# Routing products in rounded halves, one key buffer, and later ranks in a fused attention, MLP and MoE kernel

## The chip, the cores and the metric

The kernel runs on one core of a Trainium2 chip. The metric is the device time of one execution in microseconds (us). Five engines matter: TensorE (PE, matrix products), VectorE (DVE), ScalarE (ACT), GpSimdE (POOL) and SyncE (SP), whose queue here issues most of the DMA transfers. A matrix product reads a stationary operand (loaded as weights, PEld in the rows) and a moving operand, and accumulates in PSUM.

## The reference

```python
# r, k, v: (4, 8, 768, 48) f32; w, u: (8, 48); attention with a decaying state
for t in range(S):
    cur = einsum('bhd,bhe->bhde', u[None] * kt, vt)
    y[:, :, t] = einsum('bhd,bhde->bhe', rt, state + cur)
    state = w[None, :, :, None] * state + einsum('bhd,bhe->bhde', kt, vt)
# x = y as (3072, 384): one row for each token
x = (relu(x @ w_in) ** 2) @ w_out                 # w_in (384, 2048), w_out (2048, 384)
noisy = x @ w_gate + log1p(exp(x @ w_noise)) * noise   # (3072, 8)
top2, weights = best_two_of(noisy), softmax_over_the_two
out[rows] += weight * (relu(x[rows] @ w1[e]) @ w2[e])  # 8 experts, (384, 1024), (1024, 384)
```

## The kernel before, in words

**Tiling.** The 3072 tokens are 24 chunks of 128 rows, or 6 blocks (j = 0 to 5) of 512 tokens. The 384 features are three pieces (d = 0, 1, 2) of 128. Most products run on pairs of rounded numbers: an operand is a rounded high part (type fp32r) plus a rounded low part, and a product is hi*hi + hi*lo + lo*hi. Attention and routing use plain fp32 operands, of which the profile records every product as two passes.

**Stages.** A written-out list of steps (HEAD) does the attention of chunks 0 to 3 and begins the conversion of the MLP's weights into such pairs. Then comes the loop over blocks j and, in it, over 16 pieces f of the MLP's width: `mm1(j, f)` (line 501, nine products of 512 columns into `ph`, two buffers), `gsplit(j, f)` (lines 507 to 513: ACT takes relu, its square `g` and the rounded square `gh`; DVE takes `gl` = g - gh), and `mm2(j, f-2)` (line 524, nine products into `xo`, a single buffer of three PSUM banks). Behind `mm2(j-1, 15)`, in f = 1 of block j, comes `finish(j-1)` (line 531): it copies `xo` from PSUM to `x2T`, d = 0 and 2 on ACT, d = 1 on DVE. After the blocks come the experts, in units of token columns, with products of 264 to 512 columns (lines 806, 857, 889).

**What sets the order.** Nothing is scheduled at run time: each engine runs its own list in the order in which the program was written and waits on semaphores. Between `mm1` and `mm2` of each f lie two slots (32 for a block), each some nine products long. Tables give the place of every other step as a slot number with a fraction: CHUNKS for the attention of the next block, CONV_AT for the weights, ROUTE for the routing of the block before. ROUTE has three rows, of which the third is for j = 5.

**Routing.** `load_routing` (line 153) fills `gates`, 128 x 3 x 144: an identity, the gate weights and the noise weights. `r_row(j, i)` (line 549) takes the 128 tokens of chunk i: three fp32 products (line 557), with the token columns of `x2T` as weights and `gates` moving, give in one PSUM bank the transposed rows (128 columns for each d) and three partial logits (16 columns for each d). DVE adds the partial logits (`lz`, line 559), ACT copies the rows (line 560). A block has four such steps. Then DVE finds the two best experts, `r_rank` (line 658) counts places with three small products on PE, which wait for DVE's selection, and eight `r_send` scatter the rows from POOL.

**Keys.** `load(q, "k")` (line 200) brings chunk q's keys into `lk`, two buffers, from SP's queue; `pre(q)` (line 348) uses them: `pre_k` (line 370, `kp` = k * tk, on DVE for most chunks, on POOL for 4 to 8), then POOL multiplies r, k and u (line 357) and issues the load of k for chunk q + 2.

Of the kernel before, what the change touches and what calls it, by code (L numbers as in the profile page):

```python
# [8 lines left out]
F32 = mybir.dt.float32  # L9
F32R = mybir.dt.float32r  # L10
# [64 lines left out]
CLEAR = {3: (8.7, 14.7, 26.7), 4: (8.7, 14.7)}  # L75
# [18 lines left out]
def body(ctx, tc, r, k, v, w, u, w_in, w_out, w_gate, w_noise, noise, w1, w2, out):  # L94
# [58 lines left out]
    def load_routing():  # L153

        g = C["gates"] = consts.tile([P, KD, P + 2 * E], F32, name="gates")
        nc.gpsimd.tensor_copy(g[:, :, :P], ident[:, None, :].to_broadcast([P, KD, P]))
        nc.scalar.dma_start(g[:, :, P:P + E], w_gate.rearrange("(c p) e -> p c e", p=P))
        nc.scalar.dma_start(g[:, :, P + E:], w_noise.rearrange("(c p) e -> p c e", p=P))

# [25 lines left out]
    def load(q, names="rkv"):  # L185
# [3 lines left out]
        for nm in names:  # L189
            if nm == "r" and q < QD:  # L190
                t = rp[q % 2][:, :, :D]
            elif nm == "r":
                t = at.tile([P, H, D], F32, name="lr", tag="s3", bufs=1)
            elif nm == "k" and q == 0:
                t = kp[0][:, :, :D]
            elif nm == "v":
                t = at.tile([P, H, D], F32, name="lv", bufs=2)
            else:
                t = at.tile([P, H, D], F32, name="l" + nm, bufs=2)
            nc.sync.dma_start(t, SRC[nm][b, :, c * P:(c + 1) * P, :].rearrange("h s d -> s h d"))  # L200
            L.setdefault(q, {})[nm] = t
# [146 lines left out]
    def pre(q):  # L348
        a = A.setdefault(q, {})
        l = L[q]  # L350
        if q:
            pre_k(q)
        if q < QD:
            t = at.tile([P, H, D], F32, name="ra", bufs=2)
        else:
            t = at.tile([P, H, D], F32, name="rk", bufs=1)
        nc.gpsimd.tensor_mul(t, l["r"], l["k"])
        nc.gpsimd.tensor_mul(t, t, ub)
        a["rk"] = t
        load(q + 2, "k")  # L360

# [142 lines left out]
    def gsplit(j, f):  # L504
        ph = PH.pop((j, f))
        rt = m1.tile([P, BLK], F32, name="rt", bufs=1)
        nc.scalar.activation(rt, ph, AF.Relu)  # L507
        g = m1.tile([P, BLK], F32, name="g", bufs=1)
        nc.scalar.activation(g, rt, AF.Square)
        gh = m1.tile([P, BLK], F32R, name="gh", bufs=3)  # L510
        nc.scalar.activation(gh, rt, AF.Square)  # L511
        gl = m1.tile([P, BLK], F32R, name="gl", bufs=3)
        nc.vector.tensor_tensor(gl, g, gh.bitcast(F32), op=OP.subtract)  # L513
        G[j, f] = gh, gl
# [12 lines left out]
    def finish(j):  # L527
        xo = XO.pop(j)
        X2[j] = eb.tile([P, KD, BLK], F32, name="x2T", tag="s6", bufs=2)
        for d in range(KD):  # L530
            (nc.vector.tensor_copy if d == 1 else nc.scalar.copy)(X2[j][:, d, :], xo[:, d, :])

# [16 lines left out]
    def r_row(j, i):  # L549
        s = RT[j]  # L550
        if i == 0:
            s["lz"] = small("lz", [TPB, 2 * E])
        n = P + 2 * E
        pb = bank()[:, :KD * n].rearrange("p (d x) -> p d x", x=n)
        x = X2[j][:, :, i * P:(i + 1) * P]
        for d in range(KD):
            nc.tensor.matmul(pb[:, d, :], x[:, d, :], C["gates"][:, d, :], start=(d == 0), stop=(d == KD - 1),  # L557
                             skip_group_check=True)
        nc.vector.tensor_reduce(s["lz"][:, i, :], pb[:, :, P:].rearrange("p d e -> p e d"), axis=AX.X, op=OP.add)
        nc.scalar.copy(r_part(s, i), pb[:, :, :P])  # L560
# [440 lines left out]
    for j in range(NB):  # L1001
# [14 lines left out]
        if j == 0:  # L1016
            put(0.6, conv_w3, 2)
            for n in range(AW, 2 * NP):
                for at_, fn in zip(CONV_AT[n - AW], (conv_w1, conv_w2, conv_w3)):
                    put(at_, fn, n)  # L1020
            put(30.6, load_routing)
        if j == 1:
# [176 lines left out]
```

## Time and profile before

| | |
|---|---|
| median of 3 runs | 972.31 us (972.05 to 973.21) |
| the profiled execution | 972.28 us |
| its span, first to last instruction | 970.6 us |
| mean granted clock of TensorE | 0.989 |
| TensorE busy | 941.2 us, 97% |
| VectorE, ScalarE, GpSimdE busy | 543.2, 437.3, 351.3 us |

The profiled execution spends 1.7 us around its span and stands at the median of the runs. Ends of TensorE's records are modelled and products overlap, so the pace of a stretch is read from the starts: the distance from one start to the next is what a product costs. A number in brackets at the end of a row of the timeline is the idle time of that engine before it, with the instruction that ended it.

### The profile page before, as it was taken

The numbers are of one execution on the slowest core, as the hardware profiler recorded it, in microseconds if no ns is written. First come the engines' busy times: TensorE is split into PE (matmuls) and PEld (weight loads), VectorE is DVE, ScalarE is ACT, GpSimd is POOL, SyncE is SP. The second block draws the span as 40 slices with busy tenths as digits, with TensorE's granted clock in tenths as the row PEclk, the third lists the DMA queues.
The fourth block names the chain that finished last, engine by engine and source line by source line (L and its number), as shares of the span: only waits on it lengthen the run. The fifth ranks groups of instructions, "written<-read, shape, count | busy, mean of one in ns | idle before, by whom it ended". The sixth has DMA issues, their size and how long they took to land.

```text
span 970.6 us, 17617 instructions
## 1 busy us (share of the span) xinstructions
PE 941.2 (97%) x6816; PEld 812.9 (84%) x6816; DVE 543.2 (56%) x986; ACT 437.3 (45%) x797; POOL 351.3 (36%) x407
## 2 busy tenths in 40 slices
PE   6898999999999999999999999999999999999995
PEld 5676787878878878877878899989999898989985
DVE  6899955545855673683344563554545454456320
ACT  4666754434344444353555542443434444444220
POOL 5555552464563354455030353132121212212112
PEclk7999999999999999999999999999999999999998
DMA  7645449943343364442025268376555555654112
GB/s 170 162 132 151 138 121 288 271 128 82 76 114 72 87 160 131 109 98 83 0 99 127 75 141 181 96 141 135 115 101 124 103 112 118 119 101 89 21 21 36
DMA packets 193365, 112.35 MB, mean 116 GB/s; under 512 B 131792, under 2 KB 185840, under 8 KB 193264
## 3 DMA queue, kind: packets, MB, share of 16 engines
q1 hardware_dynamic: 181840, 91.22, 37.2%
q0 software_dynamic: 10624, 19.74, 11.1%
q8 instruction: 65, 1.06, 0.5%
q14 instruction: 36, 0.29, 0.1%
q10 hardware_dynamic: 800, 0.02, 0.0%
HBM read 74.83 MB, written 36.12 MB: 114 GB/s over the span
## 4 chain that ended last, share of the span: by engine, by line
PE 84%; DVE 8%; DMA 2%; ACT 2%; issue 1%; SPq 1%; POOL 0%; POOLq 0%; ACTq 0%; DVEq 0%
PE ph L806 19%; PE xo L524 17%; PE ph L501 17%; PE y L857 13%; PE y L889 4%; PE att L439 4%; PE ph L889 2%; PE att L421 2%; PE att L557 2%; PE y L806 2%; DVE t L276 1%; DVE t L275 1%; DMA stg<-in_moe_w_in 1%; DVE t L274 1%; DVE gl L513 1%
## 5 line engine op out<-in xcount | busy, mean ns | idle before, releaser
L868 POOL DMA_INDIRECT out<-yt,id x56 | 87.1, 1556 | 309.1 <-ACT yt L866 271.3
L513 DVE TENSOR_TENSOR gl<-g,gh 128x512 fp32r<-128x512 f32 x96 | 80.7, 841 | 145.2 <-ACT gh L511 141.9
L843 DVE SCALAR_TENSOR_TENSOR hl<-ph,hh 128x512 fp32r<-128x512 f32 (+1 forms) x112 | 66.6, 598 | 117.9 <-ACT hh L842 117.7
L507 ACT ACTIVATE rt<-ph 128x512 f32<-128x512 f32 x96 | 57.2, 595 | 157.8 <-PE ph L501 157.8
L806 PE MATMUL ph<-xh,w0h 128*128 128x512 f32 (+1 forms) x336 | 119.3, 355 | 0.0
L501 PE MATMUL ph<-x1h,wih 128*128 128x512 f32 x288 | 117.7, 409 | 1.3 <-ACT rt L507 0.7
L806 PE MATMUL ph<-xh,w0l 128*128 128x512 f32 (+2 forms) x336 | 116.8, 348 | 0.0
L806 PE MATMUL ph<-xl,w0h 128*128 128x512 f32 (+2 forms) x336 | 116.5, 347 | 0.2 <-DVE xl L783 0.2
L524 PE MATMUL xo<-gh,woh 128*128 128x512 f32 x288 | 114.7, 398 | 0.0
L524 PE MATMUL xo<-gh,wol 128*128 128x512 f32 x288 | 112.4, 390 | 0.9 <-POOL wol L289 0.9
L501 PE MATMUL ph<-x1l,wih 128*128 128x512 f32 x288 | 112.7, 391 | 0.1
L501 PE MATMUL ph<-x1h,wil 128*128 128x512 f32 x288 | 112.3, 390 | 0.0
L524 PE MATMUL xo<-gl,woh 128*128 128x512 f32 x288 | 112.3, 390 | 0.0
L842 ACT ACTIVATE hh<-ph 128x512 fp32r<-128x512 f32 (+1 forms) x112 | 58.6, 524 | 83.8 <-PE ph L806 83.5
L857 PE MATMUL y<-w1h,hh 128*128 128x384 f32 x256 | 85.7, 335 | 0.0
L857 PE MATMUL y<-w1l,hh 128*128 128x384 f32 x256 | 85.6, 335 | 0.0
L857 PE MATMUL y<-w1h,hl 128*128 128x384 f32 x256 | 85.6, 334 | 0.0
L685 POOL DMA_INDIRECT sent<-row,si x48 | 50.3, 1048 | 61.2 <-ACT gh L511 44.8
L806 PEld LDWEIGHTS ph<-xh,w0l 128*128 128x128 f32 x336 | 63.1, 188 | 7.9
L806 PEld LDWEIGHTS ph<-xl,w0h 128*128 128x128 f32 x336 | 63.3, 188 | 7.3 <-DVE xl L783 0.5
L806 PEld LDWEIGHTS ph<-xh,w0h 128*128 128x128 f32 x336 | 63.1, 188 | 7.0 <-ACT xh L782 0.4
L501 PEld LDWEIGHTS ph<-x1h,wih 128*128 128x128 f32 x288 | 54.0, 188 | 17.5 <-issue 2.8
(209 smaller groups left out, 2067.7 us busy)
## 6 DMA issues: line engine op xcount, KB each, us to landing
ws<-in_moe_w SPq DMA_DIRECT2D x128, 96.0 KB, 2.9
ws<-in_moe_w SPq DMA_DIRECT2D x32, 384.0 KB, 3.6
sent<-zero SPq DMA_DIRECT2D x8, 1375.5 KB, 8.3
G<-sent SPq DMA_DIRECT2D x36, 192.0 KB, 3.9
stg<-in_moe_w_in SPq DMA_DIRECT2D x8, 768.0 KB, 5.1
stg<-in_moe_w_out SPq DMA_DIRECT2D x8, 768.0 KB, 4.2
out<-zero SPq DMA_DIRECT2D x5, 960.0 KB, 5.6
lv<-in_v SPq DMA_DIRECT2D x24, 192.0 KB, 3.6
```

The costliest lines, as they stand in the source:

```text
L439: nc.tensor.matmul(pb[32 * n:32 * n + 32, d, :], x, y, skip_group_check=True, **kw)
L501: nc.tensor.matmul(ph, wt[qi][:, d, sl], xt[j][:, d, :], start=(n == 0), stop=(n == 3 * KD - 1))
L507: nc.scalar.activation(rt, ph, AF.Relu)
L513: nc.vector.tensor_tensor(gl, g, gh.bitcast(F32), op=OP.subtract)
L524: nc.tensor.matmul(XO[j][:, d, :], wt[qi][:, fo, sl], gt, start=(f == 0 and n == 0), stop=(f == NF - 1 and n == 2))
L685: st = nc.gpsimd.indirect_dma_start(out=sent, in_=s["row"][:, i, :], in_offset=None, out_offset=bass.IndirectOffsetOnAxis(ap=s["si"][:, i, ...
L806: nc.tensor.matmul(ph[:, c], wt[:, d, sl], xt[:, d, c], start=(m == 0), stop=(m == 3 * KD - 1))
L842: nc.scalar.activation(hh[:, :n], ph, AF.Relu)
L843: nc.vector.scalar_tensor_tensor(hl[:, :n], ph, 0.0, hh[:, :n].bitcast(F32), op0=OP.max, op1=OP.subtract)
L857: nc.tensor.matmul(py, ht[:, sl], wt[:, fo, :], start=(m == 0), stop=(m == 3 * NF2 - 1))
L868: st = nc.gpsimd.indirect_dma_start(out=out, in_=yt, in_offset=None, compute_op=OP.add, out_offset=bass.IndirectOffsetOnAxis(ap=IDX[e, un] ...
L889: nc.tensor.matmul(py[d][:, c], wt[:, fo, sl], ht[:, c], start=(m == 0), stop=(m == 3 * NF2 - 1))
```

## The change

1. `gates` becomes 128 x 3 x 160 in fp32r: identity, rounded gate and noise weights, and what the rounding left. Its raw weights are loaded in slot 26 of block 0 and split in slot 30 (`split_routing`: four ACT instructions, one on DVE; POOL's copy of the identity goes).
2. `finish` rounds `xo` to `x2h` (ACT) and takes the rest as `x2l` (DVE), for every d, in place of the three copies.
3. `r_row` takes six fp32r products of 160 columns in place of three fp32 products of 144, and `lz` adds six partial logits.
4. `gsplit` makes `gh` first and then squares `rt` in place; the buffer `g` goes.
5. `lk` has one buffer; the load of chunk q + 1's keys is issued in `pre(q)`, and none in `pre(0)`. The product of r and k always goes to `ra`, two buffers.
6. In block 5 the rank of block 4 and its second weight step move from slot 10 to 11, and the sends from 12.1 to 16.3 to 12.6 to 16.6.

```diff
@@ -70,8 +70,8 @@
           25.32, 26.97, 30.88, 25.84, 25.99, 21.93, 31.39, 31.66),
          (4.94, 7.82, 9.35, 9.61, 10.1, 13.34, 13.45, 13.47, 13.721, 14.31, 20.46, 19.12, 21.54,
           24.75, 22.9, 28.29, 28.16, 23.33, 24.72, 21.55, 28.65),
-         (4.22, 4.4, 5.4, 5.47, 5.64, 6.68, 7.8, 7.81, 8.7, 9.5, 9.6, 10.9, 10.6,
-          12.1, 12.7, 13.3, 13.9, 14.5, 15.1, 15.7, 16.3))
+         (4.22, 4.4, 5.4, 5.47, 5.64, 6.68, 7.8, 7.81, 8.7, 9.5, 9.6, 11.9, 11.6,
+          12.6, 13.2, 13.8, 14.4, 15, 15.6, 16.2, 16.6))
 CLEAR = {3: (8.7, 14.7, 26.7), 4: (8.7, 14.7)}
 FETCH_00 = 16.7
 TURN_00 = ((21.8, 22.8), (23.8, 24.8), (25.8, 26.8))
@@ -152,10 +152,19 @@
 
     def load_routing():
 
-        g = C["gates"] = consts.tile([P, KD, P + 2 * E], F32, name="gates")
-        nc.gpsimd.tensor_copy(g[:, :, :P], ident[:, None, :].to_broadcast([P, KD, P]))
-        nc.scalar.dma_start(g[:, :, P:P + E], w_gate.rearrange("(c p) e -> p c e", p=P))
-        nc.scalar.dma_start(g[:, :, P + E:], w_noise.rearrange("(c p) e -> p c e", p=P))
+        g = C["gates"] = consts.tile([P, KD, P + 4 * E], F32R, name="gates")
+        raw_ = eb.tile([P, KD, 2 * E], F32, name="gates_in", tag="s3", bufs=1)
+        nc.scalar.dma_start(raw_[:, :, :E], w_gate.rearrange("(c p) e -> p c e", p=P))
+        nc.scalar.dma_start(raw_[:, :, E:], w_noise.rearrange("(c p) e -> p c e", p=P))
+        C["gates_in"] = raw_
+
+    def split_routing():
+        g, raw_ = C["gates"], C["gates_in"]
+        hi = g[:, :, P:P + 2 * E]
+        for d in range(KD):
+            nc.scalar.activation(g[:, d, :P], ident, AF.Copy)
+        nc.scalar.activation(hi, raw_, AF.Copy)
+        nc.vector.tensor_tensor(g[:, :, P + 2 * E:], raw_, hi.bitcast(F32), op=OP.subtract)
 
     ident = consts.tile([P, P], F32, name="ident")
     make_identity(nc, ident)
@@ -196,7 +205,7 @@
             elif nm == "v":
                 t = at.tile([P, H, D], F32, name="lv", bufs=2)
             else:
-                t = at.tile([P, H, D], F32, name="l" + nm, bufs=2)
+                t = at.tile([P, H, D], F32, name="lk", bufs=1)
             nc.sync.dma_start(t, SRC[nm][b, :, c * P:(c + 1) * P, :].rearrange("h s d -> s h d"))
             L.setdefault(q, {})[nm] = t
 
@@ -350,14 +359,12 @@
         l = L[q]
         if q:
             pre_k(q)
-        if q < QD:
-            t = at.tile([P, H, D], F32, name="ra", bufs=2)
-        else:
-            t = at.tile([P, H, D], F32, name="rk", bufs=1)
+        t = at.tile([P, H, D], F32, name="ra", bufs=2)
         nc.gpsimd.tensor_mul(t, l["r"], l["k"])
         nc.gpsimd.tensor_mul(t, t, ub)
         a["rk"] = t
-        load(q + 2, "k")
+        if q:
+            load(q + 1, "k")
 
     def pairs(q):
         return L[q]["v"].rearrange("p (a s) d -> p a (s d)", s=2)
@@ -505,12 +512,11 @@
         ph = PH.pop((j, f))
         rt = m1.tile([P, BLK], F32, name="rt", bufs=1)
         nc.scalar.activation(rt, ph, AF.Relu)
-        g = m1.tile([P, BLK], F32, name="g", bufs=1)
-        nc.scalar.activation(g, rt, AF.Square)
         gh = m1.tile([P, BLK], F32R, name="gh", bufs=3)
         nc.scalar.activation(gh, rt, AF.Square)
+        nc.scalar.activation(rt, rt, AF.Square)
         gl = m1.tile([P, BLK], F32R, name="gl", bufs=3)
-        nc.vector.tensor_tensor(gl, g, gh.bitcast(F32), op=OP.subtract)
+        nc.vector.tensor_tensor(gl, rt, gh.bitcast(F32), op=OP.subtract)
         G[j, f] = gh, gl
 
     def mm2(j, f):
@@ -526,9 +532,12 @@
 
     def finish(j):
         xo = XO.pop(j)
-        X2[j] = eb.tile([P, KD, BLK], F32, name="x2T", tag="s6", bufs=2)
+        x2h = eb.tile([P, KD, BLK], F32R, name="x2h", tag="s6", bufs=2)
+        x2l = eb.tile([P, KD, BLK], F32R, name="x2l")
         for d in range(KD):
-            (nc.vector.tensor_copy if d == 1 else nc.scalar.copy)(X2[j][:, d, :], xo[:, d, :])
+            nc.scalar.activation(x2h[:, d, :], xo[:, d, :], AF.Copy)
+            nc.vector.tensor_tensor(x2l[:, d, :], xo[:, d, :], x2h[:, d, :].bitcast(F32), op=OP.subtract)
+        X2[j] = x2h, x2l
 
 
     RT = {}
@@ -550,13 +559,13 @@
         s = RT[j]
         if i == 0:
             s["lz"] = small("lz", [TPB, 2 * E])
-        n = P + 2 * E
+        n = P + 4 * E
         pb = bank()[:, :KD * n].rearrange("p (d x) -> p d x", x=n)
-        x = X2[j][:, :, i * P:(i + 1) * P]
         for d in range(KD):
-            nc.tensor.matmul(pb[:, d, :], x[:, d, :], C["gates"][:, d, :], start=(d == 0), stop=(d == KD - 1),
-                             skip_group_check=True)
-        nc.vector.tensor_reduce(s["lz"][:, i, :], pb[:, :, P:].rearrange("p d e -> p e d"), axis=AX.X, op=OP.add)
+            for m, x in enumerate(X2[j]):
+                nc.tensor.matmul(pb[:, d, :], x[:, d, i * P:(i + 1) * P], C["gates"][:, d, :], start=(d == 0 and m == 0),
+                                 stop=(d == KD - 1 and m == 1), skip_group_check=True)
+        nc.vector.tensor_reduce(s["lz"][:, i, :], pb[:, :, P:].rearrange("p d (s e) -> p e d s", s=2), axis=AX.XY, op=OP.add)
         nc.scalar.copy(r_part(s, i), pb[:, :, :P])
         if i == TPB - 1:
             s["lz"] = s["lz"].rearrange("p i (c e) -> p i c e", c=2)
@@ -1018,7 +1027,8 @@
             for n in range(AW, 2 * NP):
                 for at_, fn in zip(CONV_AT[n - AW], (conv_w1, conv_w2, conv_w3)):
                     put(at_, fn, n)
-            put(30.6, load_routing)
+            put(26.6, load_routing)
+            put(30.6, split_routing)
         if j == 1:
             for e in range(E):
                 put(e * 3 // 2 + 3.6, zeros, e)
```

On ACT and DVE, at `finish(1)` in block j = 2 (`gl` is gsplit's low part; the row above the copies is block j = 2's own `gsplit`). ACT before, then after:

```order
L511 ACTIVATE gh<-rt 128x512
L531 COPY x2T<-xo 128x512 [waits PE_49]
L531 COPY x2T<-xo 128x512 [waits DVE_49]
L507 ACTIVATE rt<-ph 128x512 [waits PE_49,Activation_49]
```

```order
L517 ACTIVATE rt<-rt 128x512 [waits Activation_49]
L538 ACTIVATE x2h<-xo 128x512 [waits PE_49]
L538 ACTIVATE x2h<-xo 128x512 [waits DVE_49] x2
L514 ACTIVATE rt<-ph 128x512 [waits PE_49,Activation_49]
```

DVE at the same place, before and after:

```order
L513 TENSOR_TENSOR gl<-g,gh 128x512 [waits DVE_49,PE_49,Activation_49]
L531 COPY x2T<-xo 128x512 [waits Activation_49]
L392 STREAM_TRANSPOSE kT<-rp_96 128x4x4x32 [waits DMAHW2_49,DMAHW7_49,DMAHW1_49,DMAHW0_49]
```

```order
L519 TENSOR_TENSOR gl<-rt,gh 128x512 [waits DVE_49,PE_49,Activation_49]
L539 TENSOR_TENSOR x2l<-xo,x2h 128x512 [waits Activation_49] x3
L399 STREAM_TRANSPOSE kT<-rp_96 128x4x4x32 [waits DMAHW6_49,DMAHW7_49,DMAHW5_49,DMAHW0_49]
```

Two instructions on ACT and one on DVE became three and three, each of which waits for the other engine.

On PE, the first row product of block 1 in block j = 2, before and after:

```order
L501 MATMUL ph<-x1h,wil_129 128x512
L557 MATMUL att<-gates,x2T 128x144 [waits Activation_49]
L557 MATMUL att<-gates,x2T 128x144 [waits DVE_49]
L557 MATMUL att<-gates,x2T 128x144 [waits Activation_49]
L524 MATMUL xo<-gh,woh_136 128x512
```

```order
L508 MATMUL ph<-x1h,wil_129 128x512
L566 MATMUL att<-gates,x2h 128x160 [waits Activation_49]
L566 MATMUL att<-gates,x2l 128x160 [waits DVE_49]
L566 MATMUL att<-gates,x2h 128x160 [waits Activation_49]
L566 MATMUL att<-gates,x2l 128x160 [waits DVE_49]
L566 MATMUL att<-gates,x2h 128x160 [waits Activation_49]
L566 MATMUL att<-gates,x2l 128x160 [waits DVE_49]
L530 MATMUL xo<-gh,woh_136 128x512
```

The place in the list is the same; the last product now waits for DVE's third subtraction. The other rows of a block (but the second in j = 5, which follows at once) wait only at their first product, for the bank.

On SP, the transfers of the first chunks (`rp` is r, `stg` raw MLP weights), before and after:

```order
L263 DMA stg<-in_moe_w_in 128x3x512 [waits DMAHW1_49]
L200 DMA lk<-in_k 128x8x48 [waits DMAHW2_49]
L200 DMA rp_95<-in_r 128x8x48 [waits DMAHW3_49,PE_49,Pool_49]
L263 DMA stg<-in_moe_w_in 128x3x512 [waits DMAHW4_49]
L200 DMA lk<-in_k 128x8x48 [waits DMAHW5_49,DMAHW7_49,DVE_49,Pool_49]
L200 DMA rp_96<-in_r 128x8x48 [waits DMAHW6_49,PE_49]
L200 DMA lv<-in_v 128x8x48 [waits PE_49]
L200 DMA lk<-in_k 128x8x48 [waits DMAHW0_49,DMAHW2_49,DVE_49,Pool_49]
L200 DMA lk<-in_k 128x8x48 [waits DMAHW1_49,DMAHW5_49,DVE_49,Pool_49]
```

```order
L272 DMA stg<-in_moe_w_in 128x3x512 [waits DMAHW1_49]
L209 DMA rp_95<-in_r 128x8x48 [waits DMAHW2_49,PE_49,Pool_49]
L272 DMA stg<-in_moe_w_in 128x3x512 [waits DMAHW3_49]
L209 DMA lk<-in_k 128x8x48 [waits DMAHW4_49,DMAHW7_49,DVE_49,Pool_49]
L209 DMA rp_96<-in_r 128x8x48 [waits DMAHW6_49,DMAHW5_49,PE_49]
L209 DMA lv<-in_v 128x8x48 [waits PE_49]
L209 DMA lk<-in_k 128x8x48 [waits DMAHW4_49,DVE_49,Pool_49]
L209 DMA lk<-in_k 128x8x48 [waits DMAHW0_49,DMAHW7_49,DVE_49,Pool_49]
```

The first `lk` shown before is chunk 2's and has no row after; the places of chunks 3, 4 and 5 carry those of 2, 3 and 4.

## Rows read from the trace of the kernel before

**Rows 1.** The page, parts 1 and 4: busy us (share) x instructions; shares of the chain.

```profile
PE 941.2 (97%) x6816; PEld 812.9 (84%) x6816; DVE 543.2 (56%) x986; ACT 437.3 (45%) x797; POOL 351.3 (36%) x407
...
PE 84%; DVE 8%; DMA 2%; ACT 2%; issue 1%; SPq 1%; POOL 0%; POOLq 0%; ACTq 0%; DVEq 0%
```

**Rows 2.** The chain of waits, 0 to 140 us: start us, us, what.

```profile
40.52 0.48 DVE t L274
...
120.83 1.74 PE att L439 x56
...
124.84 2.04 PE ph L501 x9
```

**Rows 3.** Timeline, all engines, start of the program: start us, us, engine line op.

```profile
13.94 0.37 SPq L200 DMA_DIRECT2D lk<-in_k  x1
...
19.65 1.02 DVE L370 TENSOR_TENSOR kp<-lk,tk 128x384 f32<-128x384 f32 x2
...
21.84 1.33 SPq L200 DMA_DIRECT2D lk<-in_k  x2
...
22.03 0.56 DVE L485 TENSOR_TENSOR x1l<-att,x1h 128x384 fp32r<-128x384 f32 x1 [1.36 <-ACT x1h L484]
...
22.64 0.86 PE L439 MATMUL att<-rT,Z 112*32 112x128 f32 x24
```

**Rows 4.** The transfers issued from 4 to 45 us: issues, KB, median us to landing.

```profile
lk<-in_k SPq DMA_DIRECT2D x6, 192.0 KB, 3.6
```

**Rows 5.** Windows, 34.6 to 38.1 us: length, busy of the engines, granted clock, DMA.

```profile
34.60:38.10 3.50, 3.50 (x55) 2.94 (x58) 2.66 (x5) 1.13 (x3) 0.45 (x1) 0.51 0.82 207
```

**Rows 6.** Timeline, block j=2, the end of block 1 (finish and its first row).

```profile
221.19 0.59 ACT L531 COPY x2T<-xo 128x512 f32<-128x512 f32 x1 [0.20 <-PE xo L524]
...
221.81 0.69 DVE L531 COPY x2T<-xo 128x512 f32<-128x512 f32 x1
...
222.53 0.59 ACT L531 COPY x2T<-xo 128x512 f32<-128x512 f32 x1 [0.76 <-DVE x2T L531]
...
223.03 0.90 PE L557 MATMUL att<-gates,x2T 128*128 128x144 f32 x6
...
223.67 0.49 PE L524 MATMUL xo<-gh,woh 128*128 128x512 f32 x1
```

**Rows 7.** Groups of instructions by shape, DVE: busy us, mean ns, idle before.

```profile
L513 DVE TENSOR_TENSOR gl<-g,gh 128x512 fp32r<-128x512 f32 x96 | 80.7, 841 | 145.2 <-ACT gh L511 141.9 <-issue 3.0
...
L843 DVE SCALAR_TENSOR_TENSOR hl<-ph,hh 128x512 fp32r<-128x512 f32 x64 | 44.1, 691 | 78.3 <-ACT hh L842 78.1
```

**Rows 8.** Timeline, the same place in j=1, then in j=5.

```profile
137.11 0.59 ACT L531 COPY x2T<-xo 128x512 f32<-128x512 f32 x1 [0.20 <-PE xo L524]
...
140.27 0.49 PE L524 MATMUL xo<-gh,woh 128*128 128x512 f32 x1
...
470.56 0.59 ACT L531 COPY x2T<-xo 128x512 f32<-128x512 f32 x1 [0.20 <-PE xo L524]
...
473.77 0.49 PE L524 MATMUL xo<-gh,woh 128*128 128x512 f32 x1
```

**Rows 9.** Timeline, the end of the last block and its row products.

```profile
536.75 0.59 ACT L531 COPY x2T<-xo 128x512 f32<-128x512 f32 x1 [4.28 <-PE xo L524]
...
540.67 1.51 PE L557 MATMUL att<-gates,x2T 128*128 128x144 f32 x11
```

**Rows 10.** Timeline, block j=5, the rank of block 4; PEld is the weight load.

```profile
487.40 0.39 PE L501 MATMUL ph<-x1h,wil 128*128 128x512 f32 x1
...
488.70 0.19 PE L658 MATMUL att<-sel,mask 128*128 128x32 bf16 x1 [0.92 <-DVE pre L622]
...
489.51 0.19 PEld L524 LDWEIGHTS xo<-gh,woh 128*128 128x128 f32 x1
...
489.53 0.48 PE L524 MATMUL xo<-gh,woh 128*128 128x512 f32 x1
...
489.62 0.19 PEld L524 LDWEIGHTS xo<-gl,woh 128*128 128x128 f32 x1
```

## The prediction

> **What bounds the kernel now.** I read the page first. TensorE is busy for 97% of the span and holds 84% of the chain that ended last; VectorE has 8% of it [rows 1]. So from one stage to another a change is worth what it does to TensorE's list, except where the chain leaves TensorE. The chain of waits says where: from 40.52 us it runs over VectorE's weight conversion, and it is back on TensorE for good at 120.83 us [rows 2]. Up to there VectorE's queue counts, behind it the distance from one TensorE start to the next; nine products of 512 columns take 2.04 us [rows 2], 0.227 each. The timeline at three places then prices the change: the head, the end of a block, the rank in block 5.
>
> All sums are made against the profiled execution, 972.28 us (1.7 of them outside its span), which is the median of the runs, 972.31, to 0.03 us.
>
> **One key buffer.** What is lost is a load. Chunk 2's keys now come at the place where chunk 3's were issued, 13.94 us. VectorE used chunk 2's keys from 19.65 us [rows 3]; the six key loads of this stretch took 3.6 us in the median [rows 4], so these land near 17.5 and this place costs nothing. Chunk 3's keys come at the place of 21.84 us, behind a load of v that waits for TensorE, and land near 21.84 + 3.6 = 25.4. VectorE did both `kp` products in one go at 19.65, 1.02 us for two [rows 3]. Now the second starts at 25.4 and ends at 26.0, and behind it in the queue stands `x1l`, which began at 22.03; TensorE went on at 22.64 only when it was done [rows 3]. That is 26.0 - 22.03 = **4.0 us** later for VectorE, and no idle time of that queue is left to take it before the conversion. If the load takes as long as chunk 2's had at most (13.94 to 19.65, 5.7 us), it is 6.0. Something comes back: from 34.6 to 38.1 us TensorE's granted clock was 0.51, the 1.2 GHz level, while transfers were dense [rows 5], and work that moves out of these 3.5 us runs up to 1.75 us shorter. So 2.2 to 6.0; I take **+3.3**, near the 4.0, since all of VectorE's work is on the chain and only some of TensorE's is. From block 1 on a chunk's keys are asked for in the step before that uses this buffer, several slots of 2.04 us ahead of their own, against 3.6 for the load: nothing. If one were late, its `kp` would hold up VectorE's queue by the difference.
>
> **Rounding at a block's end.** Before: ACT 221.19, DVE 221.81, ACT 222.53, each waiting for the last, done at 223.12; the first row's six passes start at 223.03 (0.90 us) and `xo`'s next product at 223.67 [rows 6]. The copies were just in time. After: the order listing shows ACT and VectorE in turn, three times each, each with a wait for the other engine. ACT's step has a row, 0.59 [rows 6]; a subtraction of 128x512 with a rounded result took 0.69 [rows 7], as did VectorE's copy here. With 0.03 between steps (221.19 + 0.59 to 221.81) it is 3 x (0.59 + 0.69) + 5 x 0.03 = 4.0 us, to 225.19. The sixth product needs the last half: it starts at 225.24, and with one product's 0.11 (below) `xo` resumes at 225.35, 1.68 us later than 223.67. The distance of 2.48 us from the first copy to that product is the same in j = 3 and 4, so 1.68 there too. In j = 1 the distance is 140.27 - 137.11 = 3.16, so 1.0; in j = 5, where two rows follow each other, 473.77 - 470.56 = 3.21 [rows 8]: 4.0 + 0.05 + 7 x 0.11 = 4.82, so 1.6. Together 3 x 1.68 + 1.0 + 1.6 = **+7.6**. The ends: a subtraction as short as the 0.56 of 384 columns [rows 3] takes 3 x 0.13 from each of five blocks, so 5.6; one more instruction of 0.69 ahead of the chain on VectorE adds that to each, so 11. What ACT and VectorE have queued behind (the next `gsplit`, the transposition of k) slips by 2 us; TensorE needs it only a product group of 2.04 us later, and TensorE itself waits 1.7, so it costs nothing, or 0.3 a block if that cover is gone. In the last block the copies start at 536.75 and the rows only at 540.67 [rows 9]: 4.0 us fit, no cost.
>
> **The row products.** Before, six passes cost 0.90 us where eleven cost 1.51 [rows 6, 9]: (1.51 - 0.90) / 5 = 0.122 a pass, 0.73 a row, 17.6 for 24 rows. After, each row has six products of 160 columns. No row shows an fp32r product so short. By columns it would be 160 / 512 x 0.227 = 0.071. But each carries its own weight load of 128 columns, and where TensorE had waited and loads ran freely they came 0.11 apart (489.51, 489.62) [rows 10]. I take **0.11**, the nearest row for what limits a short product. The other end: fp32 pace, two passes of 0.122 x 160 / 144 = 0.271. The six rows counted with the waits above leave 18: 18 x 6 x (0.122 - 0.11) = **-1.3** (by columns -5.5, at fp32 pace +16.1). `lz` adds twice as many elements, on a VectorE that is busy for 56% [rows 1]; nothing of TensorE's list needs it soon.
>
> **The later rank.** In block 5 a product starts at 487.40 and the next block's products at 489.53; between them TensorE waited 0.92 us and more for VectorE's selection [rows 10]. Of 489.53 - 487.40 - 0.23 = 1.90 us the three small products need 0.25, an estimate from the 0.22 that the last ones took before 489.53. So 1.65 is wait. A slot later, 2.04 us of products lie in between: **-1.65**, or -1.3 if VectorE's selection slips by 0.3 behind the longer rounding. VectorE's second weight step moves along; the sends on POOL end a third of a slot later, still before the fetch in slot 16.7.
>
> **At nothing.** `gsplit`: relu of the next f must now wait for `gl` of this one, but VectorE is waiting for ACT before nearly every `gl` (145.2 us idle for 96) [rows 7] and the next `ph` comes 4 us after the last; at most 1 us over the blocks. `split_routing` adds four small ACT steps and one on VectorE in the last slot of block 0, hidden by products; without cover about 1 us. `ra` for `rk`: a second buffer, a gain of nothing.
>
> **Sum:** 972.28 + 3.3 + 7.6 - 1.3 - 1.65 = **980.2 us**.
>
> **The rivals.** *Products by columns.* If weight loads hide beside other products, 0.071 instead of 0.11 takes 18 x 6 x 0.039 = 4.2 and 0.4 from the first rows: **975.6**. For it: the loads of a 512-column stream always overlap. Against: 0.11 was the closest that two loads came.
> The Trainium skill, "TensorE: Matmul & The Clock Gate", section "Back-to-back issue gap", gives some 81 ns for a product of 128 columns in a stream of loads and products; by it, as an estimate, the 18 rows would give 4.4 instead of 1.3, and the sum would be 977.1. No run here shows such a stream of fp32r products.
> *Fp32 pace.* If short rounded products run at the fp32 pace, 0.271, the 18 rows cost +16.1 instead of -1.3, the second row of j = 5 0.97 and the five last products 0.8 more: **999.4**. For it: nothing in the trace is both rounded and below 264 columns. Against: it would need two passes for one product.
> *No change: three low ends.* Products by columns, the load of keys at its lower end (2.2) and the short subtractions (5.6): 975.6 - 1.1 - 2.0 = **972.5**. Each end is open; all three at once are unlikely.
> *Faster: the rounding overlaps.* The place is `finish`: the order listing names only the engine waited for. If ACT's second and third rounding need not wait for VectorE's subtraction, the chain is 0.59 + 3 x 0.69 and gaps, done at 223.95, and with products by columns each of five blocks loses 0.35 instead of 1.5. Then 972.28 + 3.3 + 1.8 - 5.8 - 1.65 = **969.9**. It decides if the chain is under 2.9 us. Against: the copies of before have the same wait and obey it, 0.76 idle behind VectorE's copy [rows 6].
>
> **How the numbers follow.** Forecast 0.62 (977 to 986), by columns 0.14, fp32 pace 0.11, no change 0.07, faster 0.06. The range from 973.0 to 986.0 takes in the first two with their bounds (the head at 6.0 and one more instruction in each rounding chain would give 980.2 + 2.7 + 3.4 = 986.3) and part of the fourth, about 0.8. A measurement of this kernel can tell 0.2%, 1.9 us, from no change: faster 0.07, same 0.07, slower 0.86.
>
> **What would show it.** Behind each block's last product: ACT and VectorE in turn for 4 us, and TensorE idle some 1.7 us before a row product of `x2l` in j = 2, 3, 4. Starts of row products 0.11 apart in j = 1 to 5. `kp` of chunk 3 near 25.4 us, behind its transfer, and the first 512-column product of the MLP some 3 us later than now. No wait before the rank in block 5. It is wrong if the rows' products come at 0.07 or 0.27, or if VectorE and ACT overlap at the block's end.

## The result and the profile after

The changed kernel takes 987.0 us in the median of four runs (984.1 to 988.3), the kernel before, beside it, 972.8: a ratio of 1.0144, 95% interval 1.0129 to 1.0158. The forecast was 980.2 in 973.0 to 986.0. The direction was right; the time lies 1.0 us above the range. The profiled execution took 988.32 us, 16.0 more than the one before; this section accounts for that execution, 1.3 us above the median.

The page of the changed kernel, its span, TensorE's busy time and the lines of the chain that ended last:

```profile
span 986.5 us, 17578 instructions
...
PE 945.6 (96%) x6816; PEld 813.6 (82%) x6816; DVE 556.9 (56%) x999; ACT 451.7 (46%) x807; POOL 353.1 (36%) x406
...
PE ph L815 19%; PE xo L530 14%; PE ph L508 14%; PE y L866 13%; PE y L898 4%; PE att L446 3%; PE ph L898 2%; PE att L428 2%; PE y L815 2%; DVE t L285 2%; DMA lk<-in_k 2%; DVE gl L519 2%; PE att L566 1%; DVE t L284 1%; DVE x2l L539 1%
```

TensorE's busy time grew by 4.4 us against [rows 1] and the span by 15.9: most of the loss is idle time. A transfer (`lk`) and a subtraction (`x2l`) now have places in the chain, which they had not before.

Lining up TensorE's starts of the same product in both profiles gives the loss at each place:

| place | forecast | measured in this profile |
|---|---|---|
| head, first product of the MLP (39.98, now 42.26) | +3.3 | +2.3 |
| rounding waits, j = 1 to 5 (1.1, 1.8, 1.8, 1.8, 1.7) | +7.6 | +8.2 |
| further row products | -1.3 | -1.1 |
| rank in block 5 | -1.65 | -1.9 |
| half clock behind two of the rounding waits | 0 | +3.0 |
| wait for Z in block 4 | 0 | +1.9 |
| late weights of the first expert, block 5 | 0 | +1.1 |
| experts | 0 | +2.3 |

The eight make 15.8 of the 16.0. The first four were forecast at +7.95 and came to +7.5. The last four make 8.3, and they are the error. Of the experts' 2.3 some 1.6 is lost near 646 us of the kernel before, where a weight piece lands late (below); the rest comes in small steps, whose cause was not found.

**The end of a block** in the timeline of the changed kernel, block j = 2; it answers to [rows 6]:

```profile
224.34 0.60 ACT L538 ACTIVATE x2h<-xo 128x512 fp32r<-128x512 f32 x1
...
224.98 0.69 DVE L539 TENSOR_TENSOR x2l<-xo,x2h 128x512 fp32r<-128x512 f32 x1
...
225.70 0.60 ACT L538 ACTIVATE x2h<-xo 128x512 fp32r<-128x512 f32 x1 [0.76 <-DVE x2l L539]
...
226.33 0.69 DVE L539 TENSOR_TENSOR x2l<-xo,x2h 128x512 fp32r<-128x512 f32 x1 [0.66 <-ACT x2h L538]
...
227.06 0.60 ACT L538 ACTIVATE x2h<-xo 128x512 fp32r<-128x512 f32 x1 [0.76 <-DVE x2l L539]
...
227.69 0.69 DVE L539 TENSOR_TENSOR x2l<-xo,x2h 128x512 fp32r<-128x512 f32 x1 [0.67 <-ACT x2h L538]
...
228.44 0.34 PE L566 MATMUL att<-gates,x2l 128*128 128x160 f32 x1 [0.39 <-DVE x2l L539]
...
228.61 0.43 PE L530 MATMUL xo<-gh,woh 128*128 128x512 f32 x1
```

ACT and VectorE take turns six times, from 224.34 to 228.38: 4.0 us, as the forecast had it. The last product of `x2l` waits for the last subtraction, and `xo`'s next product starts at 228.61, where it was 223.67 before: 4.94 later, of which 3.16 was there ahead of this row, so 1.78 is lost here.

**The clock**, in windows of the changed kernel (length, busy of PE, PEld, DVE, ACT, POOL with counts, then the granted clock, DMA share, GB/s):

```profile
396.00:398.00 2.00, 1.33 (x5) 0.94 (x6) 1.42 (x2) 1.94 (x4) 0.00 (x0) 1.00 0.00 0
398.00:400.00 2.00, 2.00 (x6) 1.57 (x5) 2.00 (x3) 0.36 (x1) 1.63 (x2) 0.52 0.28 65
400.00:402.00 2.00, 2.00 (x15) 1.27 (x15) 2.00 (x1) 0.00 (x0) 2.00 (x3) 0.62 0.51 121
402.00:404.00 2.00, 2.00 (x15) 1.62 (x14) 2.00 (x3) 0.48 (x1) 1.92 (x2) 1.00 0.02 3
```

The same rounding wait in block 4 ends at 397.50. TensorE was busy for 1.33 of the 2 us around it; behind it the granted clock fell to 0.52, the 1.2 GHz level, and was back at 402. Starts in this stretch are 0.43 apart instead of 0.227, and the stretch lost 1.5 us. Block 5 shows the same from 486.8 to 490.3; blocks 1 to 3 do not.

**The keys in block 4**, the chain of waits from 420 to 470 us (start, us, what):

```profile
431.81 0.48 DVE kp L377
...
432.34 0.39 SPq L209
...
433.97 1.48 SPq L228
...
437.04 3.67 DMA rp<-in_r
...
455.28 4.10 DMA sent<-row,si
...
459.54 0.51 POOL Z L480
...
460.09 0.86 PE att L446 x22
```

From the top: VectorE's `kp` reads the one key buffer; only then may SP issue the next keys (432.34). Behind them in SP's queue stands `rp` (433.97, four transfers), which is then late. `kp` itself kept its place: in both kernels it stands in VectorE's list behind the routing steps of the block before, and now the next load in SP's queue depends on it. VectorE waits 3.49 us for `rp` before 440.79, and with it everything in its list, the routing weights among it. So POOL's sends start late, and Z, which stands behind them in POOL's list, keeps TensorE waiting until 460.09.

**The head**, timeline:

```profile
21.57 5.34 SPq L209 DMA_DIRECT2D lk<-in_k  x2
25.10 0.56 DVE L377 TENSOR_TENSOR kp<-lk,tk 128x384 f32<-128x384 f32 x1 [5.20 <-DMA lk<-in_k]
...
25.58 0.55 DVE L492 TENSOR_TENSOR x1l<-att,x1h 128x384 fp32r<-128x384 f32 x1
...
26.18 1.08 PE L446 MATMUL att<-rT,Z 112*32 112x128 f32 x16 [3.07 <-DVE x1l L492]
...
42.26 0.49 PE L508 MATMUL ph<-x1h,wih 128*128 128x512 f32 x1 [0.61 <-ACT x1h L491]
```

Chunk 3's `kp` starts at 25.10, where [rows 3] has the pair done by 20.67, and `x1l` at 25.58 instead of 22.03: 3.55 late. Of it 2.3 is left at the first product of the MLP. Some 1.3 came back on products that ran at half clock before [rows 5], from 35.2 to 37.9, and run at full clock now, from 38.8 to 40.3, though transfers are denser here:

```profile
37.90:41.40 3.50, 3.44 (x96) 3.02 (x95) 3.31 (x6) 1.82 (x3) 0.66 (x1) 1.00 0.97 253
```

This part is a matter of the execution too: of the profiles with two key buffers, the kernel before's second one has such a stretch from 34.0 to 37.4, and those of part 4 alone and of both repairs with the later fetch (below) have none there.

**The rank and what follows it**, timeline of block 5:

```profile
504.12 0.19 PE L667 MATMUL att<-sel,mask 128*128 128x32 bf16 x1
...
504.21 0.47 PE L508 MATMUL ph<-x1h,wih 128*128 128x512 f32 x1
...
527.23 0.42 SPq L733 DMA_DIRECT2D ws<-in_moe_w  x1
...
532.50 0.84 ACT L742 ACTIVATE w0h<-ws 128x768 fp32r<-128x768 f32 x1 [7.68 <-DMA ws<-in_moe_w]
...
533.88 0.50 PE L508 MATMUL ph<-x1h,wih 128*128 128x512 f32 x1 [0.83 <-ACT rt L514]
```

The three small products cost nothing now, where [rows 10] shows a wait. But the eight sends follow on POOL some 1.27 us apart, as before, and the first starts at 510.48, where it was 495.81: 14.7 later, while the products around it are 12.7 later. The weight pieces are issued at 527.23, behind the fetch of the first expert's rows, ACT's conversion waits for them, its relu stands behind the conversion, and TensorE waits for relu.

### The profile page after: what moved, and what is told of

The parts are those of the page before. It is cut to its first block, busy times and chain, and to the rows that moved or that the text cites. A ratio compares the mean times of both kernels' runs of the same rounds, so it can differ in the third digit from the quotient of the medians.

```text
span 986.5 us, 17578 instructions
## 1 busy us (share of the span) xinstructions
PE 945.6 (96%) x6816; PEld 813.6 (82%) x6816; DVE 556.9 (56%) x999; ACT 451.7 (46%) x807; POOL 353.1 (36%) x406
## 3 DMA queue, kind: packets, MB, share of 16 engines
q0 software_dynamic: 10624, 19.74, 10.9%
## 4 chain that ended last, share of the span: by engine, by line
PE 76%; DVE 11%; DMA 5%; ACT 3%; issue 2%; SPq 1%; POOL 1%; POOLq 0%; DVEq 0%; ACTq 0%
PE ph L815 19%; PE xo L530 14%; PE ph L508 14%; PE y L866 13%; PE y L898 4%; PE att L446 3%; PE ph L898 2%; PE att L428 2%; PE y L815 2%; DVE t L285 2%; DMA lk<-in_k 2%; DVE gl L519 2%; PE att L566 1%; DVE t L284 1%; DVE x2l L539 1%
## 5 line engine op out<-in xcount | busy, mean ns | idle before, releaser
L519 DVE TENSOR_TENSOR gl<-rt,gh 128x512 fp32r<-128x512 f32 x96 | 86.5, 902 | 129.6 <-ACT rt L517 129.1
```

What stands on the lines that cost most here:

```text
L519: nc.vector.tensor_tensor(gl, rt, gh.bitcast(F32), op=OP.subtract)
```

## The experiments

Each is compared with the kernel before on the same chip, whose median was 971.8 to 972.1 us.

### Two key buffers

```diff
-                t = at.tile([P, H, D], F32, name="lk", bufs=1)
+                t = at.tile([P, H, D], F32, name="lk", bufs=2)
...
-        t = at.tile([P, H, D], F32, name="ra", bufs=2)
+        if q < QD and q % 2:
+            t = eb.tile([P, H, D], F32, name="ra", tag="x2l", bufs=1)
+        else:
+            t = at.tile([P, H, D], F32, name="rk", bufs=1)
...
-        if q:
-            load(q + 1, "k")
+        load(q + 2, "k")
```

The room for the second key buffer comes from the product of r and k, which has one buffer again and shares `x2l`'s for the odd ones of the first eight chunks.

> The changed kernel, with part 5 undone: two buffers for the keys, loads two chunks ahead as before. Theory A (the single buffer costs twice: the head, where kp of chunk 3 waits for its keys, 2.3 us at the start of the blocks; and in block 4, where the load of keys stands in SP's queue until kp of the chunk before has read the buffer and r's transposed rows behind it come late, 1.9 us at POOL's Z): 987.0 - 4.2 = 982.8 us; the first product of line 501's kind starts near 40.0 us, and no wait for Z on TensorE in block 4. Rival B (only the head is the key buffer's; the late rows of r in block 4 come from the longer rounding on VectorE): 984.7 us, and the wait for Z stays.

Measured: 978.1 us (977.4 to 979.6), ratio 1.0058 [1.0035, 1.0081]: 8.9 less than the changed kernel, more than twice what theory A gave. The first product of the MLP starts at 38.91, there is no wait for Z, and `rp` is issued at 423.23 instead of 433.97, 5.4 us sooner when the 5.3 us are taken off by which TensorE's products there are ahead:

```profile
422.66 0.47 SPq L209 DMA_DIRECT2D lr<-in_r  x1
...
423.23 3.13 SPq L228 DMA_DIRECT2D rp<-in_r  x4
```

So theory A holds for both places, and its price was too small. From profile to profile the difference is 10.9 us (988.3 to 977.4), of which 10.2 can be placed: 3.3 in the head, where this execution is 1.1 ahead even of the kernel before, 1.9 at Z, 3.0 of half clock and 1.0 of late weights that the profile no longer shows, and 1.0 in the experts. The rounding waits are all still there. That the half clock and the late weights went because of the keys is not shown by this run alone: both are seen to come and go below.

### Three tiles for xo

```diff
-            XO[j] = xops.tile([P, KD, BLK], F32, name="xo")
+            XO[j] = [xops.tile([P, BLK], F32, name=f"xo{d}") for d in range(KD)]
...
-                nc.tensor.matmul(XO[j][:, d, :], wt[qi][:, fo, sl], gt, start=(f == 0 and n == 0),
+                nc.tensor.matmul(XO[j][d], wt[qi][:, fo, sl], gt, start=(f == 0 and n == 0),
...
-            nc.scalar.activation(x2h[:, d, :], xo[:, d, :], AF.Copy)
+            nc.scalar.activation(x2h[:, d, :], xo[d], AF.Copy)
-            nc.vector.tensor_tensor(x2l[:, d, :], xo[:, d, :], x2h[:, d, :].bitcast(F32), op=OP.subtract)
+            nc.vector.tensor_tensor(x2l[:, d, :], xo[d], x2h[:, d, :].bitcast(F32), op=OP.subtract)
```

> The changed kernel, with xo as three tiles of one PSUM bank each in place of one of three banks; nothing else. Theory A (ACT's roundings and VectorE's subtractions take turns because both read one tile; the wait that this makes on TensorE costs 1.1 + 4 x 1.77 = 8.2 us, and the granted clock at 0.5 behind two of these waits, in blocks 4 and 5, 2.9 more): ACT rounds without waiting for VectorE, and begins d = 0 before the last products, so no wait before the row products and no half clock there; 987.0 - 8.2 - 2.9 = 975.9 us, 974.5 to 978. Rival B (the half clock has another source than the wait): 978.8 us with a stretch at 0.5 still in blocks 4 or 5. Rival C (the row products themselves are what costs): no change.

Measured: 977.9 us (976.7 to 978.1), ratio 1.0050 [1.0033, 1.0067], 9.1 less than the changed kernel, inside theory A's range. The timeline of block 2's end:

```profile
223.12 1.55 ACT L538 ACTIVATE x2h<-xo 128x512 fp32r<-128x512 f32 x3
...
223.85 1.88 DVE L539 TENSOR_TENSOR x2l<-xo,x2h 128x512 fp32r<-128x512 f32 x3
...
225.25 0.27 PE L566 MATMUL att<-gates,x2l 128*128 128x160 f32 x1
...
225.36 0.28 PE L566 MATMUL att<-gates,x2h 128*128 128x160 f32 x1
...
225.97 0.43 PE L530 MATMUL xo<-gh,woh 128*128 128x512 f32 x1
```

ACT's three roundings run in 1.55 us without a wait between them, VectorE's in 1.88 beside them. From the first rounding to the last subtraction, at 225.73, it is 2.6 us instead of 4.0. The row products start before that; the first five come 0.08 to 0.11 apart, and only the sixth, at 225.79, waits some 0.1 us for the last subtraction. No microsecond of the profile from 60 to 960 has a lower clock. The turns were a dependence through one tile, not a limit of the two engines. Head, Z and late weights are still in this profile (2.2, 2.2 and 0.8).

### The rank back, and the fetch later

```diff
-         (4.22, 4.4, 5.4, 5.47, 5.64, 6.68, 7.8, 7.81, 8.7, 9.5, 9.6, 11.9, 11.6,
-          12.6, 13.2, 13.8, 14.4, 15, 15.6, 16.2, 16.6))
+         (4.22, 4.4, 5.4, 5.47, 5.64, 6.68, 7.8, 7.81, 8.7, 9.5, 9.6, 10.9, 10.6,
+          12.1, 12.7, 13.3, 13.9, 14.5, 15.1, 15.7, 16.3))
```

> The changed kernel, with the third row of ROUTE as before: rank in slot 10, sends from 12.1. Theory A (moving the rank saves its wait, 1.9 us, but the eight sends follow each other on POOL without a gap and start 2.0 us later against the products, so the first expert's fetch, the weight loads behind it on SP and the ACT conversion behind them are late, 1.1 us of TensorE's waiting in block 5): the wait of 1.9 comes back and the 1.1 goes, 987.0 + 0.8 = 987.8 us. Rival B (the late conversion has another source): 987.0 + 1.9 = 988.9 us with both waits.

Measured: 987.8 us (984.4 to 988.8), ratio 1.0156 [1.0133, 1.0179]. The time doesn't separate the theories; the profile has the rank's wait again (1.00 us before the first small product and 0.42 before the second) and none for the late weights, which is A. The profiled execution took 984.4 us, and no half clock shows behind its rounding waits.

```diff
-FETCH_00 = 16.7
+FETCH_00 = 16.9
```

> The changed kernel, with the fetch of the first expert's rows in slot 16.9 instead of 16.7, so that the load of a weight piece of slot 16.8 stands ahead of it in SP's queue. Theory A (the weights are late because they stand behind the fetch, which waits for the last send): ACT's conversion in block 5 is no longer late and TensorE's wait of 1.1 us for relu goes, 987.0 - 1.1 = 985.9 us. Rival B (the weights wait for their buffer, not for the place in the queue): no change, 987.0.

Measured: 987.2 us (986.4 to 987.8), ratio 1.0146 [1.0124, 1.0168]: as B gave. But the profile shows TensorE's wait for relu gone, as A gave, and beside the half clock in block 4 a stretch at 0.5 from 660 to 664, behind a wait in the experts, that the changed kernel's profile lacks. The total is no judge here; both edits were tried again on a kernel without the large waits.

### Both repairs, and the two edits on top

The first two diffs together:

> The changed kernel with both: two key buffers, and xo as three tiles. Theory A (the two costs are apart: the keys 8.9 us, as two buffers gave alone; the rounding 7.4 to 9 us, of which some is half clock that falls away with either): 987.0 - 8.9 - 7.4 = 970.7 us, between 969.5 and 972; what stays against the kernel before is the rank's 1.9 and the row products' 1.2 to 1.7 as gain, and some 1 us late in the experts as loss. Rival B (two buffers and three tiles remove the same wait): 977.

Measured: 970.7 us (970.1 to 971.2, 12 runs), ratio 0.9986 [0.9977, 0.9996]. Theory A's number. Alone the repairs save 8.9 and 9.1, together 16.3: they share some 2 us. No half clock is left in the profile from 60 to 960 us. Late weights are left (0.7):

```profile
511.05 1.37 SPq L735 DMA_DIRECT2D ws<-in_moe_w  x3
...
516.43 0.85 ACT L744 ACTIVATE w0h<-ws 128x768 fp32r<-128x768 f32 x1 [7.29 <-DMA ws<-in_moe_w]
...
517.81 0.50 PE L510 MATMUL ph<-x1h,wih 128*128 128x512 f32 x1 [0.43 <-ACT rt L516]
```

With the fetch at 16.9 besides:

> As the run with two key buffers and three tiles, and the fetch of the first expert's rows in slot 16.9, behind the load of a weight piece. Theory A (with the keys in time the sends and the conversion of block 5 are in time too): the same time as without. Rival B (the late conversion comes from the rank's new place): 1 us less.

Measured: 969.8 us (968.3 to 970.5, 12 runs), ratio 0.9976 [0.9965, 0.9987]: 0.8 less, B. This is the fastest version of all. In its timeline a piece of weights goes ahead of the fetch and the conversion is not late:

```profile
501.75 1.76 SPq L735 DMA_DIRECT2D ws<-in_moe_w  x4
...
507.17 2.04 SPq L770 DMA_DIRECT2D G<-sent  x3
...
508.06 0.84 ACT L744 ACTIVATE w0h<-ws 128x768 fp32r<-128x768 f32 x1
```

With the rank back instead:

> As the run with two key buffers and three tiles, with the rank of block 4 back in slot 10 and the sends from 12.1. Theory A (with everything else in time the rank's wait of 1.65 to 1.9 us is all that the place decides): 1.7 us more, near 972.4. Rival B (the sends' later start costs 1.1 in block 5, so that the later rank gains only 0.8): 0.8 more.

Measured: 971.8 us (970.4 to 975.4, 12 runs), ratio 0.9997 [0.9985, 1.001]: 1.1 more than with the later rank. That lies between A's 1.7 and B's 0.8. With the run before: the later rank gives some 1.9 and takes 0.8 back in the weights.

### The key buffer alone

In the kernel before:

```diff
-                t = at.tile([P, H, D], F32, name="l" + nm, bufs=2)
+                t = at.tile([P, H, D], F32, name="lk", bufs=1)
...
-        load(q + 2, "k")
+        if q:
+            load(q + 1, "k")
```

> The kernel before, with part 5 alone: one key buffer, loads one chunk ahead. Theory A (the buffer's own cost is 2.3 to 3.4 us in the head and 1.9 us in block 4, and with no long rounding on VectorE nothing else): 972.1 + 4.2 to 5.3 = 976.3 to 977.4 us, with a wait for Z in block 4. Rival B (the late r of block 4 needs the long rounding as well): 974.4 to 975.5 us, without that wait. Rival C (the keys cost 8.9 here as in the changed kernel): 981.

Measured: 978.7 us (977.5 to 980.6), ratio 1.0069 [1.0052, 1.0086]: 6.9 more, above A's 4.2 to 5.3 and below C. The timeline of block 4:

```profile
424.53 0.55 DVE L371 TENSOR_TENSOR kp<-lk,tk 128x384 f32<-128x384 f32 x1
...
425.14 0.38 SPq L200 DMA_DIRECT2D lk<-in_k  x1
...
426.76 1.49 SPq L219 DMA_DIRECT2D rp<-in_r  x1
...
433.96 1.09 DVE L393 STREAM_TRANSPOSE rT<-rp 128x512 f32<-128x512 f32 x1 [3.87 <-DMA rp<-in_r]
...
452.53 0.41 PE L440 MATMUL att<-rT,Z 112*32 112x128 f32 x2 [0.81 <-POOL Z L474]
```

The late `rp` and the wait for Z are there without any longer rounding, so B falls. Of this 6.9 the prediction had 3.3. The profiled execution took 977.45; it shows 1.7 to 2.1 in the head, 2.5 in block 4 and 0.9 in the experts. What the other five lose beyond was not seen; their mean granted clock is 0.984 to 0.988 against 0.989, so some of it may be half clock.

### The clock behind a longer wait

```diff
-            nc.scalar.activation(x2h[:, d, :], xo[:, d, :], AF.Copy)
+            for _ in range(2):
+                nc.scalar.activation(x2h[:, d, :], xo[:, d, :], AF.Copy)
```

> The changed kernel, with every rounding of finish done twice, so that the chain behind a block's last product is 3 x 0.6 us longer and TensorE waits some 3.5 us before the row products of blocks 1 to 5 instead of 1.7. Theory A (the waits before the row products bring TensorE's clock to half behind them, some times in five): 5 x 1.85 = 9.3 us more wait, and a stretch at 0.5 behind most of the five, 1.45 us for each that the changed kernel did not have: 987.0 + 9.3 + 2 to 4.4 = 998.3 to 1000.7 us. Rival B (the half clock has nothing to do with the waits): 996.3 us, with at most the two stretches of the changed kernel.

Measured: 1006.8 us (1005.1 to 1008.4), ratio 1.0362 [1.0345, 1.0380], more than either. Windows of blocks 2 and 3, the wait and then what follows:

```profile
230.00:234.50 4.50, 1.89 (x8) 1.28 (x8) 2.25 (x3) 3.62 (x7) 0.00 (x0) 1.00 0.00 0
234.50:239.00 4.50, 4.50 (x25) 3.31 (x24) 4.50 (x3) 0.23 (x1) 4.26 (x4) 0.62 0.34 84
318.00:321.00 3.00, 0.81 (x3) 0.37 (x2) 0.69 (x1) 2.18 (x5) 0.00 (x0) 0.84 0.00 0
321.00:327.00 6.00, 5.75 (x19) 4.21 (x21) 6.00 (x4) 1.72 (x3) 4.19 (x4) 0.51 0.24 60
```

All five blocks now have a stretch near 0.5 behind the wait, some 3.5 us long in blocks 1 and 2 and some 6 to 7 in blocks 3 to 5. Theory A's mechanism holds and its price was too small. Against the changed kernel's profile the five waits cost 1.6 to 1.9 us more each, as the theory had it. The half clock costs 1.5 us a block in blocks 1 and 2 and 2.3 to 2.9 in blocks 3 to 5, where 1.45 was put on each; and the rows of the last block, which no theory counted, wait 1.9.

### The two kernels again, and part 4 alone

> The changed kernel once more, for a second profile. Theory A (half clock behind the rounding waits comes and goes from one execution to the next, and the waits themselves stay): 987 us median in 984 to 989, waits of 1.7 us before the row products in blocks 2 to 5, and a number of stretches at 0.5 behind them that may differ from two. Rival B (they belong to blocks 4 and 5): two again, behind the same waits.

Measured: 987.2 us (984.6 to 989.4), ratio 1.0164 [1.0138, 1.019]. The second profile has the same waits and one stretch at half clock, in block 5; A, though with two profiles only the block 4 stretch is seen to come and go. The profiled execution (985.5) has a mean granted clock of 0.988; of the three without a profile those of 989.0 and 989.4 have 0.981 and 0.982, that of 984.6 has 0.990. So half clock probably came more often in the longer two; this is not shown.

> The kernel before once more, for a second profile. Theory A (the microsecond that every run since lost near 646 us, where an expert's weight piece lands late, is a matter of the execution and not of the change, since the kernel before with one key buffer lost it too): the second profile may show that piece landing later than the first did, with TensorE waiting more than 0.2 us for xh there. Rival B (it belongs to the change): the first profile's picture again. Time: no change, 972.

Measured: 972.0 us, ratio 1.0002 [0.9992, 1.0012]. The place near 646 us, in the second profile of the kernel before:

```profile
646.68 0.50 PE L806 MATMUL ph<-xh,w0h 128*128 128x512 f32 x1 [0.35 <-ACT xh L782]
```

and in the changed kernel:

```profile
653.18 0.85 ACT L742 ACTIVATE w1h<-ws 128x768 fp32r<-128x768 f32 x1 [4.01 <-DMA ws<-in_moe_w]
...
661.71 0.50 PE L815 MATMUL ph<-xh,w0h 128*128 128x512 f32 x1 [1.01 <-ACT xh L791]
```

The kernel before loses 0.4 us more there than in its first profile, the changed kernel 1.6 in its first profile and 0.6 in its second, for a weight piece that lands late. It is a matter of the execution in part; whether the change adds to it stays open.

Part 4 in the kernel before:

```diff
-        g = m1.tile([P, BLK], F32, name="g", bufs=1)
-        nc.scalar.activation(g, rt, AF.Square)
         gh = m1.tile([P, BLK], F32R, name="gh", bufs=3)
         nc.scalar.activation(gh, rt, AF.Square)
+        nc.scalar.activation(rt, rt, AF.Square)
...
-        nc.vector.tensor_tensor(gl, g, gh.bitcast(F32), op=OP.subtract)
+        nc.vector.tensor_tensor(gl, rt, gh.bitcast(F32), op=OP.subtract)
```

> The kernel before, with part 4 alone: the rounded square first, then the square in place of relu, no buffer for it. Theory A (it costs nothing, since VectorE's subtraction is done before the next relu in nearly every f): no change, 971.8 us, within 1. Rival B (relu's new wait for VectorE's subtraction costs in block 0, where VectorE is the bound): 1 to 3 us more.

Measured: 973.0 us (971.1 to 974.6), ratio 1.0010 [1.0001, 1.0020]: 1.2 more, outside A's microsecond and of B's size. But its profile has no new wait in block 0 or any other, where B had it. What it loses is 1.4 us in the experts, at the place near 646 us:

```profile
647.04 0.50 PE L805 MATMUL ph<-xh,w0h 128*128 128x512 f32 x1 [1.01 <-ACT xh L781]
```

That is the changed kernel's wait of 1.01, in a kernel without its rounding, its key buffer and its ranks. So this wait needs none of those parts; whether part 4 makes it more frequent is open.

## Why the prediction was right in part and wrong in its range

**The rounding at a block's end** was right in mechanism and size: 4.0 us of turns, 1.7 to 1.8 a block, 8.2 against 7.6. The three tiles took the wait away and, in their profile, the half clock behind it.

**The row products** were right: 0.11 apart, the distance of the weight loads in [rows 10], against 0.071 by columns and 0.271 at the fp32 pace. The rule that the prediction set against it (the Trainium skill, "TensorE: Matmul & The Clock Gate", "Back-to-back issue gap": some 81 ns at 128 columns) was not met by these products of 160 columns in fp32r; the measurement decides.

**The head** was right in mechanism, 3.55 at `x1l` and 2.3 at the MLP's first product, against 4.0 and 3.3. What the prediction expected to come back there, work that leaves the stretch of half clock, did come back, some 1.3; but that stretch itself comes and goes, so the size of the 2.3 is in part chance.

**The rank** gave 1.9 against 1.65. But the step that put the sends at nothing ("still before the fetch in slot 16.7") failed: they follow each other on POOL without a gap, so their start, 2.0 us later against the products, moves their end, the fetch behind them and the weights behind the fetch on SP. The two runs with both repairs put 0.8 us on it.

**The step that failed most, by the experiments,** is the one that priced the keys "from block 1 on" at nothing, because they are asked for slots ahead. It asked when the keys are needed and not who stands behind them. The load of keys was not late for its own use; it held SP's queue until `kp` had read the buffer, and r's rows behind it came late. This cost 1.9 to 2.5 us in block 4, in the changed kernel and in the kernel before with one buffer alone, where the whole of part 5 cost 6.9 against the 3.3 forecast.

**The clock** had no term. The prediction read a half clock only in the head [rows 5] and priced a wait of TensorE at its length; behind two of the five new waits it cost 1.5 us more each. In the profiled execution this is the largest single term of the error, 3.0.

The rivals fell: no products by columns, none at the fp32 pace, and ACT and VectorE do take turns. The sum of what was priced, +7.5, would have fitted; what was priced at nothing and the clock took the time out of the range. Of that 8.3 the runs trace 6.0 to the clock, Z and the late weights; of the experts' 2.3 the greater part is a wait that other kernels show as well, and the rest stays open.

## What to carry to other kernels

When a buffer is taken away, look at the queue that its load stands in, not only at the load's own slack: a transfer that waits for its buffer holds up all that were written behind it. When two engines share the reading of a PSUM result, give each bank a tile of its own; the turns disappear (2.6 us for the chain here instead of 4.0). Price a new wait of TensorE at more than its length, since the clock may fall behind it, and judge small edits on a version that has no such waits.

## What was not expected of the hardware

A wait with three short row products in it, some 1.7 us long, left the clock at full in some blocks and halved it for 3 to 3.5 us in others: two of five waits in one profile of the changed kernel, one in the next, one with the fetch later, and none in the profiles with two key buffers and with the rank back, which have the same waits. With the rank back the profiled execution had a mean granted clock of 0.990 (984.4 us); that kernel's other three, 987.1 to 988.8 us at 0.982 to 0.985, probably had some. Longer waits, 3.5 us, halved it five times of five, for up to 7 us. In the kernel before, a wait of 0.9 us and more at the rank had not done it: granted 1.00 from 485 to 492 us around the place of [rows 10]. Why some of the equal waits did and others did not is open.
